# Attention and routed experts on one core: TensorE's program for 24 attention steps becomes a loop

## Chip, cores and metric

The kernel runs on one core of a Trainium2 chip. The metric is device time in microseconds, from one launch to its end. Each engine (TensorE for matmuls, VectorE, ScalarE, GpSimd, and SyncE, which issues DMAs) runs a program of its own; the programs meet at semaphores.

## What is computed

Attention inside chunks of 64 positions, then a two-level top-1 mixture of experts over the 4608 rows that attention gives.

```python
B, H, S, D = 8, 8, 576, 64; chunk = 64
scores = (1 / sqrt(D)) * matmul(q_c, k_c.T)          # per chunk of 64
attn = exp(scores - max); attn /= attn.sum(-1) + 1e-09
x = matmul(attn, v_c) -> (B * S, H * D) = (4608, 512)
g_idx = argmax(x @ w_group); g_w = softmax(...)[g_idx]           # 4 groups
e_idx = argmax(x[g] @ w_expert[g]); e_w = softmax(...)[e_idx]    # 4 experts in each
out[tok] = g_w * e_w * (relu(x[tok] @ w1[g, e]) @ w2[g, e])      # 512 -> 1024 -> 512
```

## The kernel before

The 4608 rows are 36 tiles of 128 rows, two chunks of 64 each. Four tiles make a group g, for which routing is done together. Attention runs as a software pipeline written out by hand: a recorder (R) takes every operation in one fixed order, puts it into the program of its engine, and works out from the memory that it reads and writes which semaphores it must wait for. Step t issues, in this order, work of several tiles:

- b(t+1), L578: scores of tile t+1 on TensorE, 16 matmuls of 64x64 (32 records, as f32 passes twice), into one of two score banks
- n(t-3), L622 to L633: VectorE divides the value product of tile t-3 by its sums and writes x
- s(t), L586 and L590: VectorE's maximum and subtraction for tile t
- c(t-1), L602: TensorE transposes the weights of tile t-1, ScalarE copies them (pT, L604)
- tile_e(t), L665 when t is odd, L672 when it is even: router matmuls, and ScalarE's copy of them
- p(t-2), L615: TensorE's product with v for tile t-2, into the one pair of output banks (ob)
- e(t): ScalarE's exponential (L596), and the exponential of routing (L691) when one is due
- x(t-3), L645: TensorE transposes x of tile t-3, ScalarE copies it (xT, L646)
- in one step of four the rank matmuls 3(g), L763 to L768, in one expert position for each row

Routing itself is a generator, route(g), then place(g), on VectorE; the calls more() slip one of its operations at a time between those of n and s, and four at a step's end. GpSimd scatters each finished tile to the memory of its experts (L801) and writes token numbers (L631). From step 24 on (EXTRA) the first expert's weights are loaded and split (F, P). Then come a written-out TAIL for the last tiles and a loop over expert tiles with branches by the tile's kind (L1144, L1128, L1090 and their second layers).

q and k come in pairs of tiles, 1 MB a load, into seven slots (NQ = 7); v comes three chunk columns a load into two buffers of nine (NV = 2). SyncE issues these loads in the recorder's order, each when its slot is free. The HEAD string is the order at the start, VS says at which step each v load stands.

TensorE's program for all of this is straight code, some 6,800 instructions. The class Pages plays it: it cuts the program into pages of 256 instructions, if it can in front of a b or p group with a wait, and jumps to the next page from there:

```python
if i > at and ops[i].stage and ops[i].waits:
    cut = i, n
...
if cut and cut[1] > room - SLACK and cut[1] < room:
    i, n = cut
...
self.pe.addr_align(PAGE, offset=0, max_nops=0)
```

## Time and profile before

| | us |
|---|---|
| median of three timed runs | 613.39 |
| lowest, highest | 613.26, 618.44 |
| profiled execution | 618.42 |
| its span, first to last instruction | 616.8 |
| TensorE busy (share of span) | 579.8 (94%) |
| VectorE busy | 360.8 (58%) |
| ScalarE busy | 263.3 (43%) |
| GpSimd busy | 158.2 (26%) |
| steps 9 to 32 of attention | 88.69 |

The profiled execution is one of its own, 5.0 us above the median. Its rows name the engine (PE is TensorE's matmuls, PEld its weight loads, DVE VectorE, ACT ScalarE, POOL GpSimd), the line of the kernel, what is written and read, and in brackets how long the engine stood idle before, with what released it as the view infers it. [...]

### The profile page before, as it was taken

The numbers are of one execution on the slowest core, as the hardware profiler recorded it, in microseconds if no ns is written. First come the engines' busy times: TensorE is split into PE (matmuls) and PEld (weight loads), VectorE is DVE, ScalarE is ACT, GpSimd is POOL, SyncE is SP. The second block draws the span as 40 slices with busy tenths as digits, with TensorE's granted clock in tenths as the row PEclk, the third lists the DMA queues.
The fourth block names the chain that finished last, engine by engine and source line by source line (L and its number), as shares of the span: only waits on it lengthen the run. The fifth ranks groups of instructions, "written<-read, shape, count | busy, mean of one in ns | idle before, by whom it ended". The sixth has DMA issues, their size and how long they took to land.

```text
span 616.8 us, 16000 instructions
## 1 busy us (share of the span) xinstructions
PE 579.8 (94%) x5711; PEld 498.9 (81%) x5712; DVE 360.8 (58%) x688; ACT 263.3 (43%) x367; POOL 158.2 (26%) x252
## 2 busy tenths in 40 slices
PE   7889979978998999999999999999999999999995
PEld 4666657756887989888889989889989988898984
DVE  4577869776767482136697474726326578763211
ACT  2455545756336241223685252626116355452111
POOL 0002314665403111212323312122111124321120
PEclk9899889997998999999999999999999999999999
DMA  7998997876549693118298763643613586921110
GB/s 280 422 312 277 352 366 240 243 228 207 163 146 395 240 330 109 39 30 296 103 348 311 261 245 121 221 153 113 236 51 123 208 323 223 331 105 64 34 44 24
DMA packets 43104, 128.27 MB, mean 208 GB/s; under 512 B 4590, under 2 KB 4974, under 8 KB 41136
## 3 DMA queue, kind: packets, MB, share of 16 engines
q1 hardware_dynamic: 32192, 93.93, 43.9%
q0 software_dynamic: 10864, 33.64, 15.5%
q8 instruction: 37, 0.61, 0.4%
q14 instruction: 11, 0.09, 0.1%
HBM read 106.40 MB, written 21.93 MB: 208 GB/s over the span
## 4 chain that ended last, share of the span: by engine, by line
PE 71%; DVE 11%; DMA 7%; issue 5%; POOL 2%; SPq 1%; ACT 1%; another core or an unknown queue 0%; DVEq 0%; POOLq 0%; ACTq 0%
PE banks L1159 28%; PE banks L1144 22%; PE banks L1128 4%; PE banks L615 2%; DVE x L633 2%; DVE pr L590 2%; DMA xgr<-xs 2%; DVE m L586 2%; DMA w1r<-in_moe_w_dram 2%; DMA qk<-in_qk_dram 2%; PE banks L471 2%; PE banks L602 2%; PE banks L1044 2%; PE banks L645 1%; PE banks L578 1%
## 5 line engine op out<-in xcount | busy, mean ns | idle before, releaser
L1144 PE MATMUL banks<-big,w1h 128*128 128x256 f32 x896 | 128.1, 283 | 1.4 <-issue 1.4
L1144 PEld LDWEIGHTS banks<-big,w1h 128*128 128x128 f32 x896 | 117.3, 192 | 2.9 <-issue 1.9
L1305 ACT ACTIVATE big<-banks 128x512 fp32r<-128x512 f32 x58 | 34.5, 596 | 158.9 <-PE banks L1144 126.0
L1159 PE MATMUL banks<-big,big 128*128 128x512 f32 x360 | 84.7, 393 | 0.0
L1635 POOL DMA_INDIRECT out_dram<-xl,io__154 x37 | 41.1, 1112 | 152.9 <-DVE xl L1371 144.4
L1159 PEld LDWEIGHTS banks<-big,big 128*128 128x128 f32 x360 | 66.5, 188 | 14.4 <-ACT big L1355 0.7
L1404 DVE SCALAR_TENSOR_TENSOR big<-banks,big 128x512 fp32r<-128x512 f32 x54 | 36.1, 687 | 64.3 <-ACT big L1305 62.0
L1159 PE MATMUL banks<-w2h,big 128*128 128x512 f32 x288 | 72.6, 399 | 0.2 <-ACT big L1305 0.2
L1144 PE MATMUL banks<-big,w1l 128*128 128x256 f32 x448 | 72.3, 283 | 0.6 <-DVE w1l L1381 0.6
L1381 DVE TENSOR_TENSOR w1l<-w1r,w1h 128x2048 fp32r<-128x2048 f32 x28 | 63.1, 2291 | 16.0 <-ACT w1h L1292 14.3
L1371 DVE TENSOR_SCALAR xl<-banks,io__154 128x512 f32<-128x512 f32 x33 | 24.7, 749 | 68.2 <-PE banks L1159 68.2
L1159 PEld LDWEIGHTS banks<-w2h,big 128*128 128x128 f32 x288 | 53.8, 190 | 12.2 <-ACT big L1305 0.9
L1144 PEld LDWEIGHTS banks<-big,w1l 128*128 128x128 f32 x448 | 61.9, 192 | 0.8 <-DVE w1l L1381 0.8
L1292 ACT CAST w1h<-w1r 128x2048 fp32r<-128x2048 f32 x28 | 52.2, 1903 | 7.8 <-DMA w1r<-in_moe_w_dram 6.0
L578 PE MATMUL banks<-qk 64*64 64x64 f32 x1152 | 27.8, 232 | 12.5 <-DMA qk<-in_qk_dram 3.5
L578 PEld LDWEIGHTS banks<-qk 64*64 64x64 f32 x1152 | 22.3, 141 | 20.8 <-DVE pr L590 4.5
L1385 DVE TENSOR_TENSOR w2l<-w2r,w2h 128x1024 fp32r<-128x1024 f32 x32 | 37.1, 1220 | 2.3 <-ACT w2h L1324 1.7
L1159 PE MATMUL banks<-w2l,big 128*128 128x512 f32 x144 | 35.6, 389 | 0.0
L604 ACT COPY pT<-banks 128x512 f32<-128x512 f32 x36 | 21.1, 586 | 33.6 <-PE banks L602 30.2
L615 PEld LDWEIGHTS banks<-va,pT 64*64 64x64 f32 x1152 | 21.4, 141 | 16.5 <-issue 4.8
L801 POOL DMA_INDIRECT xs<-x,pos x24 | 24.2, 1008 | 40.3 <-DVE pos L810 21.7
L1629 POOL COPY in__155<-xgr 128x2 int32<-128x2 int32 x22 | 10.7, 485 | 92.6 <-PE banks L1044 78.7
(223 smaller groups left out, 906.8 us busy)
## 6 DMA issues: line engine op xcount, KB each, us to landing
w1r<-in_moe_w_dram SPq DMA_DIRECT2D x30, 1024.0 KB
w2r<-in_moe_w_dram SPq DMA_DIRECT2D x30, 1024.0 KB
qk<-in_qk_dram SPq DMA_DIRECT2D x15, 1024.0 KB, 17.4
xgr<-xs POOLq DMA_DIRECT2D x38, 257.0 KB, 5.6
va<-in_v_dram SPq DMA_DIRECT2D x24, 390.0 KB
qk<-in_qk_dram SPq DMA_DIRECT2D x6, 512.0 KB, 8.7
w1r<-in_moe_w_dram POOLq DMA_DIRECT2D x2, 1024.0 KB, 9.4
w2r<-in_moe_w_dram POOLq DMA_DIRECT2D x2, 1024.0 KB, 8.2
```

What stands on the lines that cost most here:

```text
L578: R.tensor.matmul(sc[cols, x, hp * CH:hp * CH + CH], lhsT=T[rows, 0, hp, cols], rhs=T[rows, 1, hp, cols], start=True, stop=True)
L615: R.tensor.matmul(o[cols, x, hp * W:hp * W + W], lhsT=pT[rows, hp, cols], rhs=v_at(2 * t + c)[rows, hp], start=True, stop=True)
L1128: m = pe.matmul(ph[n], a_[:, c, 0:P], w_[:, c, n * 512:(n + 1) * 512], start=(i == 0), stop=(i == 11))
L1144: m = pe.matmul(ph[f // 2][:, f % 2 * 256:f % 2 * 256 + 256], w_[:, c, f * P:(f + 1) * P], a_[:, c, :], start=(i == 0), stop=(i == 11))
L1159: m = pe.matmul(py[j], a_[:, f, half[j]], w_(b, f), start=(i == 0), stop=(i == 23))
L1292: lambda b, s, j: ac.copy(wt[b][0][:, s], w1r[j]), K1)
L1305: ac.activation(hth()[:, 2 * b:2 * b + 2, :], ph[b].rearrange("p (f t) -> p f t", f=2), AF.Relu).then_inc(S["Ha"], 1)
L1371: return ve.tensor_scalar(out=yb[:, j, :], in0=py[j], scalar1=io_[:, j, 1:2], scalar2=None, op0=ALU.mult)
L1381: lambda b, s, j: ve.tensor_sub(wt[b][1][:, s], w1r[j], wt[b][0][:, s].bitcast(F32)), K1, js)
L1385: m = ve.tensor_sub(wt[b][4 + 2 * j + i], w2r[j][:, 2 * i:2 * i + 2], wt[b][2 + j][:, 2 * i:2 * i + 2].bitcast(F32))
L1404: ve.scalar_tensor_tensor(out=htl()[:, 2 * b:2 * b + 2, :], in0=ph[b].rearrange("p (f t) -> p f t", f=2), scalar=0.0, in1=hth()[:, 2 * b:2 ...
L1635: gp.indirect_dma_start(out, bass.IndirectOffsetOnAxis(ap=io[:, j, 0:1].bitcast(I32), axis=0), yb[:, j, :], None, bounds_check=N - 1, oob_ ...
```

## The change

TensorE's steps 9 to 32 are emitted once, as a loop of three turns of eight steps (play_turns). All operations must then be alike in each turn, or alike in turns of the same parity: stretches that differ stand in an if with two branches; these are the x transposes, since the x buffers of four groups fill two turns. Page cuts are gone; the loop starts on a page. Waits inside the loop can't count upward over turns, so they become tokens: take(name, o) makes the next TensorE operation wait until a semaphore of its own is 1 (16 for a DMA), and takes that much off it again; it stands in every turn, needed or not.

The tokens: BR, the score bank is free (VectorE's subtraction, passed on by ScalarE through a relay ahead of its exponential); XT, at c, ScalarE's copy of the x transposes of the step before; VX, at x, VectorE's x; PS and PT for the rank bank; the DMA of v at c of odd tiles, the DMA of the next q, k pair at p of even tiles.

So that turns are alike, the rings change: q and k in four slots (NQ = 4, 7 before), v in one ring of 16 chunk columns, four a load (NV = 16), its layout transposed on the host to match. HEAD and VS follow. In the step, p(t-2) is issued after x(t-3) instead of ahead of e(t).

In routing three operations of VectorE per group are folded. The comparison with the maximum (L707) goes into the next operation, which compares the difference with 0; the added 1e-9 (L743) becomes a fifth column of the exponentials; the running sum (L748) becomes a fifth row of the one-hot matrix (ohs), summed with it. The rank matmuls of odd groups have one small count matmul more.

```diff
-NV = 2
-NQ = 7
+NV = 16
+NQ = 4
+T0, T1, TURN = 9, 33, 8
 RE = RPE + 1
 XW = D + 2
 
...
-HEAD = "q0 I0 q1 V0 q2 q3 V1 q4 q5 V2 I1 G0 Q3 V3 Q4 V4 Q5 V5 Q6"
+HEAD = "q0 I0 q1 v0 q2 q3 v1 q4 q5 V1 I1 G0 Q3 V2 V3"
...
-VS = {}
-for _n in range(3 * NV, 3 * B):
-    VS.setdefault((3 * _n + 2 - 9 * NV) // 2 + 2, []).append(_n)
+VS = {2 * n - 5: (n,) for n in range(NV // 4, NT // 2)}
...
+    def take(self, name, o, via=None):
+
+        self.due.append((name, o, via))
+
+    def relay(self, eng, name, o):
+
+        op = Op(eng, None, None)
+        op.at, op.token, op.passes, op.line = len(self.ops[eng]), name, True, sys._getframe(1).f_lineno
+        self.want(op, [o])
         self.ops[eng].append(op)
...
-class Pages:
...
+    def play_turns(self, pe):
+        ops, turns = self.ops["tensor"], self.turns
+        first, n = ops.index(turns[0][0]), len(turns[0])
+        for op in ops[:first]:
+            self.emit("tensor", pe, op)
+        pe.addr_align(PAGE, offset=0, max_nops=0)
+        owed = []
+        with pe.Fori(0, len(turns)) as k:
+            odd = self.tc.nc.snap(k % 2, min_val=0, max_val=1)
+            at = 0
+            while at < n:
+                to, alike = at, turns[0][at].sig == turns[1][at].sig
+                while to < n and (turns[0][to].sig == turns[1][to].sig) == alike:
+                    to += 1
+                if alike:
+                    for op in turns[0][at:to]:
+                        self.emit("tensor", pe, op, owed)
                 else:
+                    with pe.If(odd == 0):
+                        for op in turns[0][at:to]:
+                            self.emit("tensor", pe, op, owed)
+                    with pe.Else():
+                        for op in turns[1][at:to]:
+                            self.emit("tensor", pe, op, owed)
+                at = to
+        for op in ops[first + n * len(turns):]:
+            self.emit("tensor", pe, op)
...
-                lane = "q%d" % (taken[0] % NQ)
-                st["T", n] = slot(qslots).rearrange("p (i z h t) -> p i z h t", i=2, z=2, h=4)
-                R.sync.dma_start(st["T", n], qk[n], lane=lane)
+                st["T", n] = qslots[n % NQ].rearrange("p (i z h t) -> p i z h t", i=2, z=2, h=4)
+                st["Q", n] = R.sync.dma_start(st["T", n], qk[n], lane="q%d" % (n % NQ))
...
-                return vbufs[b % NV][:, j]
-
-            def load_v(n):
-
-                b, i = divmod(n, 3)
-                R.sync.dma_start(vbufs[b % NV][:, 3 * i:3 * i + 3], v[b, :, 3 * i:3 * i + 3], lane="v%d" % (n % (3 * NV)))
+                return va[:, cc % NV]
+
+            def load_v(n, lo=0, hi=4, lane="v%d"):
+
+                i = 4 * n % NV
+                st["V", n] = R.sync.dma_start(va[:, i + lo:i + hi], v[:, 4 * n + lo:4 * n + hi], lane=lane % (n % (NV // 4)))
+
+            def load_v_half(i):
+
+                load_v(0, 2 * i, 2 * i + 2, "w%d%%d" % i)
 
...
                 T = st["T", t // 2][:, t % 2]
-                R.tensor.stage("b%d" % t)
                 sc = scb[t % 2]
+                if T0 < t <= T1:
+                    R.take("BR%d" % (t % 2), st[t - 2]["told"], st[t - 2]["sub"])
...
             def stage_exp(t):
                 pr = st[t]["pr"]
+                if T0 < t + 2 <= T1:
+                    st[t]["told"] = R.relay("scalar", "BR%d" % (t % 2), st[t]["sub"])
                 R.scalar.activation(pr, pr, AF.Exp, scale=0.125)
...
                 for hp in range(4):
+                    if T0 <= t + 1 < T1 and hp == 0:
+                        R.take("XT%d" % (t % 2), st[t - 3]["xt"])
+                    if T0 <= t + 1 < T1 and t % 2 and hp == 1:
+                        R.take("v%d" % (t // 2 % (NV // 4)), st["V", t // 2])
                     R.tensor.transpose(pt[:, hp, :], s["pr"][:, hp].rearrange("p x k -> p (x k)"), ident)
                 pT = apool.tile([P, 4, P], F32, name="pT")
-                R.scalar.copy(pT, pt)
+                s["pt"] = R.scalar.copy(pT, pt)
...
                 for hp in range(4):
                     for x, c, rows, cols in TILES:
+                        if T0 <= t + 3 <= T1 and t % 2 == 0 and (hp, x, c) == (1, 0, 0):
+                            R.take("q%d" % ((t // 2 + 2) % NQ), st["Q", t // 2 + 2])
                         R.tensor.matmul(o[cols, x, hp * W:hp * W + W], lhsT=pT[rows, hp, cols], rhs=v_at(2 * t + c)[rows, hp], start=True, stop=True)
...
                 for c in range(4):
+                    if T0 <= t + 3 < T1 and c == 0:
+                        R.take("VX%d" % (t % 2), st[t]["x_"])
                     R.tensor.transpose(pt[:, c, :], s["x"][:, c * P:(c + 1) * P], ident)
-                R.scalar.copy(st["xT", g][:, :, i * P:(i + 1) * P], pt)
+                s["xt"] = R.scalar.copy(st["xT", g][:, :, i * P:(i + 1) * P], pt)
 
...
+                        if T0 <= t + 4 < T1 and t % NG == 3 and c == 1:
+                            R.take("PS%d" % (t // NG % 2), st["ps", t // NG - 1])
                         R.tensor.matmul(e[32 * c:32 * c + 32, :], lhsT=wg[:, c, :], rhs=st["xT", g][:, c, i * P:i * P + 2 * P],
...
-                one = rpool.tile([P, R5, 4], F32, name="one")
-                V.tensor_tensor(out=by_t(one), in0=L, in1=by_t(mb), op=ALU.is_equal)
                 ls = rpool.tile([P, R5, 4], F32, name="ls")
                 V.tensor_tensor(out=by_t(ls), in0=L, in1=by_t(mb), op=ALU.subtract)
                 yield
 
-                io = cs[:, C_IOTA4:C_IOTA4 + 4].unsqueeze(1).broadcast_to([P, R5, 4])
-                V.scalar_tensor_tensor(out=one, in0=one, scalar=-64.0, in1=io, op0=ALU.mult, op1=ALU.add)
-                ex = rpool.tile([P, R5, 4], F32, name="ex")
-                st["ex"] = ex, ls
+                io = cs[:, C_I16:C_I16 + 4].unsqueeze(1).broadcast_to([P, R5, 4])
+                one = rpool.tile([P, R5, 4], F32, name="one")
+                V.scalar_tensor_tensor(out=one, in0=ls, scalar=0.0, in1=io, op0=ALU.is_equal, op1=ALU.mult)
+                ex = exs[g % 2]
+                st["ex"] = ex[:, :, 0:4], ls
...
-                        V.tensor_scalar(out=gt, in0=sv[:, :, 0:2], scalar1=1e-9, scalar2=None, op0=ALU.add)
+                        V.reciprocal(gt, sv[:, :, 0:2])
                     yield
-                with nc.allow_low_precision(reason="a sum of four ones and zeros"):
-                    V.tensor_reduce(out=cum[:, g + 1, :], in_=oh.rearrange("p t g e -> p (g e) t"), axis=AX.X, op=ALU.add)
-                V.reciprocal(gt, gt)
-                V.tensor_tensor(out=cum[:, g + 1, :], in0=cum[:, g + 1, :], in1=cum[:, g, :], op=ALU.add)
+                with nc.allow_low_precision(reason="a sum of ones and zeros, at most 36"):
+                    V.tensor_reduce(out=ohs[(g + 1) % 2][:, 0], in_=oh5.rearrange("p t e -> p e t"), axis=AX.X, op=ALU.add)
...
+                if T0 <= g * NG + 10 < T1:
+                    R.take("PT%d" % (g % 2), st[g * NG + 9]["pt"])
                 R.tensor.matmul(rk3, lhsT=one1, rhs=wide(cs[0:1, C_BASE:C_BASE + E], NG), start=True, stop=False)
-                R.tensor.matmul(rk3, lhsT=ones, rhs=wide(cum[:, g, :], NG), start=False, stop=False)
+                R.tensor.matmul(rk3, lhsT=ones, rhs=wide(ohs[g % 2][:, 0], NG), start=False, stop=False)
...
+                if g % 2 and g < GL - 1:
+                    n = rk[0:1, NG * E:NG * E + E]
+                    R.tensor.matmul(n, lhsT=ones[:, 0:1], rhs=ohs[(g + 1) % 2][:, 0], start=True, stop=True)
                 if g == GC:
...
                 for t in range(TL - 2):
+                    R.turn = (t - T0) // TURN if T0 <= t < T1 else None
                     run("b%d n%d s%d c%d" % (t + 1, t - 3, t, t - 1) if t > 2 else ("b1 s0", "c0 b2 s1", "p0 b3 s2 c1")[t])
                     if 4 <= t <= 4 + (GL - 1) * NG:
                         tile_e(t)
-                    run("p%d" % (t - 2) if t > 2 else "")
                     more(4)
                     run("e%d" % t)
                     stage_ex()
                     if t % 2 and t // 2 + NQ < NT // 2:
                         run("Q%d" % (t // 2 + NQ))
                     run("x%d" % (t - 3))
+                    run("p%d" % (t - 2) if t > 2 else "")
                     run(" ".join("V%d" % n for n in VS.get(t, ())))
                     if last(t - 7):
                         run("3%d" % ((t - 7) // NG))
                     run(EXTRA.get(t, ""))
+                R.turn = None
                 run(TAIL)
...
-                    Pages(pe, R).play(lambda op: R.emit("tensor", pe, op))
+                    R.play_turns(pe)
```

## Rows read from the trace of the kernel before

**Rows 1.** The 24 steps by windows: busy us (records), clock, DMA share, GB/s

```profile
45.73:48.72 2.99, 2.99 (x83) 2.11 (x81) 1.99 (x7) 1.58 (x4) 0.00 (x0) 1.00 0.96 295
48.72:51.50 2.78, 2.78 (x77) 2.45 (x76) 2.65 (x8) 1.94 (x5) 0.00 (x0) 1.00 0.65 253
51.50:54.50 3.00, 3.00 (x82) 2.12 (x81) 2.96 (x13) 1.91 (x5) 0.00 (x0) 1.00 0.62 140
54.50:57.98 3.48, 3.45 (x85) 2.94 (x84) 2.87 (x11) 2.04 (x5) 1.50 (x2) 1.00 0.94 278
57.98:64.84 6.86, 5.48 (x83) 3.47 (x81) 3.29 (x11) 2.18 (x5) 2.91 (x5) 0.77 1.00 401
...
84.90:89.38 4.48, 4.48 (x80) 2.98 (x80) 2.79 (x15) 1.49 (x3) 0.42 (x1) 0.62 0.98 398
...
sum 88.69, PE 78.34 PEld 60.26 DVE 67.22 ACT 48.76 POOL 32.07; mean PE 3.26 PEld 2.51 DVE 2.80 ACT 2.03 POOL 1.34
```

**Rows 2.** TensorE's timeline: start, length, engine, line, [idle before it <- releaser]

```profile
27.79 0.69 PE L578 MATMUL banks<-qk 64*64 64x64 f32 x32 [1.41 <-DVE m L586]
...
39.35 0.69 PE L578 MATMUL banks<-qk 64*64 64x64 f32 x32 [1.84 <-DVE x L633]
...
72.30 0.69 PE L578 MATMUL banks<-qk 64*64 64x64 f32 x32 [1.50 <-DVE pos L810]
...
79.15 0.70 PE L615 MATMUL banks<-va,pT 64*64 64x65 f32 x32 [1.62 <-issue]
...
84.90 0.69 PE L578 MATMUL banks<-qk 64*64 64x64 f32 x32 [1.68 <-DVE xl L633]
...
106.92 0.69 PE L578 MATMUL banks<-qk 64*64 64x64 f32 x32 [0.84 <-DVE ps L785]
...
112.50 0.70 PE L615 MATMUL banks<-va,pT 64*64 64x65 f32 x32 [0.95 <-DVE mx L702]
```

**Rows 3.** DMA queues in the 24 steps: packets, MB, share of 16 engines

```profile
q8 instruction: 16, 0.26, 1.3%
```

**Rows 4.** DMA queues from 69.80 to 70.90 us

```profile
q8 instruction: 1, 0.02, 5.7%
```

**Rows 5.** DMA packets from 16.5 to 39.35 us

```profile
DMA packets 1911, 9.39 MB, mean 411 GB/s; under 512 B 212, under 2 KB 274, under 8 KB 1058
```

**Rows 6.** VectorE's timeline near the end of the 24 steps

```profile
125.97 0.69 DVE L633 TENSOR_TENSOR x<-banks,rc 128x512 f32<-128x512 f32 x1 [2.42 <-POOL x L631]
```

**Rows 7.** All DMA queues that moved anything from 295 us to the end

```profile
q1 hardware_dynamic: 16000, 41.95, 36.9%
q0 software_dynamic: 4856, 13.82, 12.0%
```

**Rows 8.** The page's costliest groups: busy us, mean ns, idle before them

```profile
L1144 PE MATMUL banks<-big,w1h 128*128 128x256 f32 x896 | 128.1, 283 | 1.4 <-issue 1.4
```

**Rows 9.** Timeline of all engines around the step at 48.72

```profile
47.51 0.70 PE L615 MATMUL banks<-va,pT 64*64 64x65 f32 x32
...
50.10 0.69 DVE L590 TENSOR_TENSOR pr<-banks,m 128x512 f32<-128x512 f32 x1
...
50.83 0.63 ACT L596 ACTIVATE pr<-pr 128x512 f32<-128x512 f32 x1
...
51.45 0.27 ACT L691 ACTIVATE ex<-ls 128x80 f32<-128x80 f32 x1
...
51.62 0.57 ACT L646 COPY xT<-banks 128x512 f32<-128x512 f32 x1
...
52.13 0.66 PE L602 MATMUL banks<-cs,pr 128*128 128x128 f32 x4
```

**Rows 10.** The page's DMA issues: count, KB each, median us to landing

```profile
qk<-in_qk_dram SPq DMA_DIRECT2D x15, 1024.0 KB, 17.4
```

**Rows 11.** Groups by line in the 24 steps: busy us, mean ns, idle before

```profile
L707 DVE TENSOR_TENSOR one<-lg,mx 128x80 f32<-128x80 f32 x5 | 1.3, 264 | 0.2
...
L748 DVE TENSOR_TENSOR cum<-cum 128x16 bf16<-128x16 bf16 x6 | 1.0, 159 | 0.0
```

More of the change, by code (lines that the diff above doesn't have):

```diff
@@ L251, in number @@
         self.sem = dict(given)
+        self.turns = {}
+        for op in self.ops["tensor"]:
+            if op.turn is not None:
+                self.turns.setdefault(op.turn, []).append(op)
+        names = set(self.eaten)
+        for same in zip(*self.turns.values(), strict=True):
+            assert len({tuple(o.takes) for o in same}) == 1
+            for o in same:
+                o.inc = any(z.inc for z in same)
+                names.update(o.takes)
+        for e in self.ENGINES:
+            for op in self.ops[e]:
+                for i, (o, val) in enumerate(op.waits):
+                    if o.token and o.lane is None:
+                        o = next(z for z in self.ops[o.eng][o.at:] if z.token is None and z.lane is None and z.fn)
+                        assert o.eng != e or o.at < op.at, (op.line, o.line)
+                        op.waits[i] = o, val
+                        if o.turn is None:
+                            o.inc = True
+                        else:
+                            assert o.inc
         for e in self.ENGINES:
@@ L272, in emit @@
             z = op.fn(eng)
-        for w in last:
-            z._wait_ge(*self.wait(*w))
+        if owed and not op.inc and not last:
+            z.then_inc(*owed.pop(0))
+        for w, n in last:
+            z._wait_ge(*w)
+            if n:
+                owed.append((w[0], n))
         if op.lane is not None:
             z.then_inc(self.sem[op.lane], 16)
+        elif op.token:
+            z.then_inc(self.sem[op.token], 1)
         elif op.inc:
@@ L355, in f @@
             z.plain = True
-            if self.name == "tensor":
-                z.cost = 4 if op == "matmul" and named["lhsT"].dtype == F32 else 2
+            z.sig = (op,) + tuple((a.tensor.name, str(a.offset), str(list(a.ap)), str(a.dtype)) for a in writes + reads)
+            z.sig += tuple((k, v) for k, v in named.items() if isinstance(v, bool))
             return z
@@ L385, in moe_kernel @@
         pos8 = wpool.tile([P, NG], I32, name="pos8")
-        cum = wpool.tile([P, NG0 + 1, E], BF16, name="cum")
+        ohs = [wpool.tile([P, NG + 1, E], BF16, name="oh%d" % i) for i in range(2)]
         ones = wpool.tile([P, P], BF16, name="ones")
@@ L398, in moe_kernel @@
         slots, qslots = [], []
-        for i in range(NQ):
+        for i in range(7):
             at_ = wpool.at
```

129 lines of the change are left out of this document (69 added, 60 removed).

## The prediction

> **What bounds the kernel now.** I looked first at the clock and span of the core (618.4 us for the profiled execution, span 616.8, mean clock 0.982), then cut the 24 steps that the change turns into a loop at the start of each score group of TensorE (L578), read that table step by step, then TensorE's timeline for what stands before each group, then the DMA queues in narrow windows around the gaps, and last the timeline of all engines in steps where TensorE never waits.
>
> Four steps in a row run undisturbed [rows 1]: 2.99, 2.78, 3.00 and 3.48 us, 12.25 together, with TensorE busy for all but 0.03 of them and VectorE for 10.5 (1.99, 2.65, 2.96, 2.87). So TensorE sets the pace of these steps, and VectorE is the next limit, full only in the third. Six times 12.25 is 73.5 us; the 24 steps took 88.69. What has to be explained is the 15.2 us between.
>
> The idle time lies in front of some groups only [rows 2]: in the loop's steps five of them, at 72.30, 79.15, 84.90, 106.92 and 112.50, wait 1.50, 1.62, 1.68, 0.84 and 0.95 us, 6.6 together; ahead of them three, from 27.79 to 39.35 (those two stand in the rows), wait 1.41, 1.02 and 1.84, 4.3 together. The view names VectorE as the releaser of most, but VectorE's work had ended earlier or ended by chance; what these eight groups have in common is in the code. The class Pages cuts TensorE's program every 1.5 steps, in front of a score or a value group, and by its cuts all eight are the first of a page. The instruction queue agrees: 16 packets of 16 KB in the 24 steps, one for each 1.5 [rows 3]. One of them starts and ends between 69.80 and 70.90, and TensorE goes on at 72.30, 1.4 us after it [rows 4]; windows around the packets ahead of 79.15 and 84.90 give the same, three in all. So TensorE runs dry at a page's end whenever the packet is late. It is late where the DMA engines are full: from 16.5 to 39.35 they move 411 GB/s [rows 5], and there three of four page starts wait a microsecond or more. In the four undisturbed steps they move 140 to 295 [rows 1], and the page starts at 48.72 and 53.28 don't wait.
>
> Two more stretches belong to it. The step at 57.98 is a page's first too, and takes 6.86 us where 2.99 would do, 3.87 too much, partly at half clock (0.77 in the row). The step at 84.90 has no gap inside but a granted clock of 0.62 after the gaps ahead of it, and costs 4.48 for 2.99, 1.49 more [rows 1]. With the five gaps that is 12.0 of the 15.2. Of the rest 1.5 us is one wait at the end: VectorE stands 2.42 us until GpSimd, behind its weight work, writes a token number [rows 6].
>
> **The change part by part.** *The loop.* A turn holds eight steps. The four undisturbed steps hold 327 matmul and 322 weight-load records [rows 1], so a turn holds some 1,300 instructions, with the second branch's copies of the x transposes about 1,400, or 5.5 pages of 256. Three turns then need some six pages instead of 16, if the code stays. The row that bears on this is the experts' loop: from 295 us to the end the instruction queue moved nothing at all, only the two data queues stand in the list [rows 7], and by the program's instruction count that loop, all its branches taken again and again, is some 1,440 instructions, a little more than the new one. So the code of turns two and three should be there. Gain: the late pages of turns two and three all go. In the first turn, and in steps 3 to 8, pages still arrive one by one, but behind lighter traffic: the load order now starts with four q, k pairs and sixteen v columns instead of seven pairs and eighteen, then loads as it consumes. From the page starts that didn't wait under such traffic I keep only 0.9 of the 4.3 us ahead of the loop (gain 3.4; ends 0 and 4.3) and 1.5 us in the first turn (ends 0 and 3.9, which is what the step at 57.98 lost), and take the 12.0 as gone.
>
> [...]
>
> *Branches.* Eight if-branches a turn around the x transposes and one jump back. No row shows a branch in these steps. The nearest are the expert matmuls at L1144, in a loop with such branches: 1.4 us of idle with no releaser over 896 matmuls [rows 8]. Each branch here stands behind the c and e groups, already queued, which hide it; that cover is thin only where a turn ends behind a value group. Between 0 and 2.4 us (0.1 at each of 24); I take 0.5, near the row.
>
> *The new order and the new wait.* In the loop the x transposes go ahead of the value group, so a value group now ends its step. Everything that VectorE does for the next tile (n, then s) starts at that end. And the weight transposes (L602) of step t+1 now wait, in every step, for ScalarE's copy of the x transposes of step t (the XT token); before, they needed only the exponential. ScalarE's own order is weight copy, logit copy, exponential, then x copy, so that copy is its last work of a step. The undisturbed step at 48.72 gives the lengths [rows 9]: from the end of a value group (47.51 + 0.70 = 48.21) to the end of the subtract (50.10 + 0.69 = 50.79) 2.58 us; the exponential follows at 50.83 for 0.63; in one step of four the routing exponential follows (51.45, as soon as ScalarE is free); the x copy runs 51.62 to 52.19. Counted from the value group's end that is 3.98 us, 4.05 with the hand-over of 0.06. With the value group last, TensorE starts the next step right at that end and reaches the transposes after a step of 2.78 and a score group of 0.63 (51.50 to 52.13), at 3.41. It waits 0.64. Behind it in TensorE's queue are the transposes, e, x and the value group, and for that value group VectorE waits, so the delay is passed on. In the following step VectorE is full (2.96) and starts some 0.25 late, which makes another 0.2 to 0.3; in the step with the rank matmuls (3.48) and the one after it the slack covers it. I take 0.88 for four steps, 5.3 for 24. Ends: 0, if ScalarE is ahead of this timeline, and 1.75 for four, 10.5 in all, if the relay that ScalarE now carries for the score banks and the later start of VectorE add 0.1 in each step and both late steps double. This wait is next late when the pages are gone.
>
> *Rings.* q, k now run four pairs ahead, v eight tiles. A pair is issued some 6.5 steps, 21 us, before it is asked for, and lands in a median of 17.4 us when seven are in flight and the queue is full [rows 10]. Four steps need 2.1 MB of q and k, 1.06 of v and 1.05 of scattered tokens; over 13.1 us that is 320 GB/s, under the 411 of [rows 5]. I cost it at nothing; SP issues them in the order in which the slots come free, with one v load behind each q load.
>
> *Three routing operations folded* (the comparison, the added constant, the running sum): 0.26, 0.19 and 0.16 us, once in four steps (the first and the last of them in [rows 11]). VectorE has over 1.7 us free in four steps, and in the stretch where it is full the routing exponential starts when ScalarE is free, not when VectorE is. Nothing, at most 0.6 for four steps, 3.7 in all, should VectorE bind.
>
> **The sum.** Against the profiled execution: 618.4 - 3.4 - 12.0 + 1.5 + 0.5 + 5.3 = 610.3. That execution lies 5.0 us over the median of 613.4, and one of the three timed runs lies there too. If the 5.0 are gaps that the change takes away (the 3.87 at 57.98 looks like it), the changed kernel comes out at 610; if they lie elsewhere, at 605. I take 609.
>
> **The rivals.** (a) The x copy is not waited for: ScalarE's chain has more slack than the one step shows. Then 5.3 less: 604. For it, the copy was never in the way before; against it, the timeline leaves it 0.6 short. (b) The late pages are not what TensorE waits for, or the first turns and other waits fill the gaps: no gain, the new wait paid: 613.4 + 5.3 + 0.5 = 619. Against it stand the eight cuts and the packet times. (c) Slower: the loop's code is not kept. Every page is fetched as before, and at two jumps back the page is asked for only then. Two stalled page starts in a row are 5.75 us apart (79.15 and 84.90), so a page from asking to use costs up to that: 2 x 5.7 + 5.8 + 613.4 = 631. It decides from the point where a turn is longer than what stays; against it, the experts' loop. (d) The wait chain takes 1.75 for four steps: 5.2 more, 614.
>
> **How the numbers follow.** The forecast, 604 to 613 by its own ends, has 0.58; (a) 0.22, (d) 0.07, (b) 0.08, (c) 0.05. A measurement of this kernel can tell 1%, 6.1 us, from no change. Below 607.3 lie three tenths of the forecast and nearly all of (a): 0.37. Above 619.5 lie (c) and half of (b): 0.09. The rest, 0.54, is within 1%. For eight in ten the range goes from 600 to 618; it leaves out (c), half of (b) and the far end of (a).
>
> **What would show it.** Right: one instruction packet for each 1.5 steps in the first turn, none in the next two; no gap with a restart 1.4 us behind a packet; rank matmuls (L763) 13.1 us apart instead of 12.25 undisturbed or 14.8 (88.69 / 6) on average; the weight transposes released by ScalarE's x copy in the step after each routing exponential. Wrong: rank groups 12.3 apart (then a), instruction packets in the second turn (c), transposes waiting in every step (d), gaps as before with no packet near (b), or waits for q or v, which I cost at nothing.

## The result and the profile after

The changed kernel took 621.97 us (median of four, 619.87 to 623.55) where the kernel before took 613.33 beside it: a ratio of 1.014 [1.010, 1.018], slower by more than the 1% that can be told from no change. Run again later it took 626.03 beside 616.06, 1.013 [1.009, 1.017]. The forecast was 609, within 600 to 618. The kernel before is not always at 613: over five chips its median went from 610.9 to 616.9 and its runs on one chip spread over 6 to 11 us, so below each kernel is read against the kernel before that was timed beside it. A ratio and its interval leave out runs more than 1.5% above the fastest of the same kernel, which the median counts: a_no_jump's 620.9 and 626.9 (of twelve runs), a_all's 630.6 and 630.8 (of six; its median is 621.7 without them), and one run each of a_one_memset, a_ex_later and the kernel before in experiment 5.

The profiled execution of after took 621.43 us (span 619.8). Its attention looks much as forecast. In the timeline of TensorE (start, length, line, tile) the rank groups, one in four steps, answer to the steps of [rows 1]:

```profile
46.17 0.43 PE L848 MATMUL banks<-cs,one 1*128 1x64 f32 x2
62.34 0.43 PE L848 MATMUL banks<-cs,one 1*128 1x64 f32 x2
76.07 0.43 PE L848 MATMUL banks<-cs,one 1*128 1x64 f32 x2
89.01 0.43 PE L848 MATMUL banks<-cs,one 1*128 1x64 f32 x2
103.02 0.43 PE L848 MATMUL banks<-cs,one 1*128 1x64 f32 x2
120.29 0.43 PE L848 MATMUL banks<-cs,one 1*128 1x64 f32 x2
```

They lie 12.9 to 17.3 apart; before they lay 12.2 to 17.7 apart. The branch records of the loop put its three turns at 38.1, 69.6 and 95.8 us, its end at 127.2. The DMA queues in turns two and three, 69.85 to 127.24, carry one packet of code on q8, at 73.7, without a stop of TensorE there (packets, MB, share of the engines); before, [rows 3] had 16 for the 24 steps:

```profile
q1 hardware_dynamic: 1906, 10.10, 53.9%
q0 software_dynamic: 2216, 7.78, 39.5%
q8 instruction: 1, 0.02, 0.1%
q14 instruction: 2, 0.02, 0.1%
```

Two things went otherwise: a stop at the loop's entry and, long after attention, a chain from VectorE and GpSimd to TensorE in the experts' loop. They stand, with the new wait of the weight transposes, in the timeline of all engines (in brackets the idle time before and what ended it):

```profile
38.42 0.89 PE L647 MATMUL banks<-qk 64*64 64x64 f32 x21 [3.23 <-issue]
...
97.77 0.66 PE L677 MATMUL banks<-cs,pr 128*128 128x128 f32 x4 [0.64 <-ACT xT L724]
...
100.97 0.66 PE L677 MATMUL banks<-cs,pr 128*128 128x128 f32 x4 [0.30 <-ACT xT L724]
...
109.99 0.62 ACT L550 CAST w1h<-w1r 128x512 fp32r<-128x512 f32 x1 [3.02 <-DMA w1r<-in_moe_w_dram]
...
112.89 1.11 PE L677 MATMUL banks<-cs,pr 128*128 128x128 f32 x4 [2.13 <-ACT xT L724]
...
157.61 0.20 PE L1272 MATMUL banks<-cs,off 1*17 1x2 f32 x2
...
297.23 4.49 DVE L1469 TENSOR_TENSOR w1l<-w1r,w1h 128x2048 fp32r<-128x2048 f32 x2 [0.83 <-issue]
...
297.32 3.11 POOL L1723 DMA_INDIRECT out_dram<-xl,io__152  x1 [2.48 <-DVE xl L1465]
...
299.70 2.56 SPq L529 DMA_DIRECT2D w1r<-in_moe_w_dram  x2
...
300.43 0.55 POOL L1769 DMA_DIRECT2D word<-xs  x1
...
306.05 0.68 POOL L1717 COPY io__152<-in__153 128x2 int32<-128x2 int32 x1 [5.07 <-DMA word<-xs]
...
309.89 0.58 POOL L1712 DMA_DIRECT2D xgr<-xs  x1 [0.77 <-POOL in__153 L1718]
...
318.12 0.75 PE L1132 MATMUL banks<-identr,xgr 128*128 128x128 f32 x4 [5.36 <-DMA xgr<-xs]
```

The same places in the timeline of the kernel before (rows that the prediction didn't show):

```profile
162.65 0.20 PE L1184 MATMUL banks<-cs,off 1*17 1x2 f32 x2
...
302.30 2.33 DVE L1381 TENSOR_TENSOR w1l<-w1r,w1h 128x2048 fp32r<-128x2048 f32 x1 [0.91 <-issue]
...
302.30 1.03 POOL L1635 DMA_INDIRECT out_dram<-xl,io__154  x1 [2.21 <-DVE xl L1377]
303.34 0.55 POOL L1681 DMA_DIRECT2D word<-xs  x1
...
304.80 2.58 SPq L459 DMA_DIRECT2D w1r<-in_moe_w_dram  x2
...
308.35 0.58 POOL L1624 DMA_DIRECT2D xgr<-xs  x1 [0.77 <-POOL in__155 L1630]
...
315.44 2.32 POOL L1635 DMA_INDIRECT out_dram<-xl,io__154  x1 [5.77 <-DVE xl L1371]
...
317.43 0.89 PE L1044 MATMUL banks<-identr,xgr 128*128 128x128 f32 x8
...
507.40 3.09 POOL L1635 DMA_INDIRECT out_dram<-xl,io__154  x1 [2.80 <-DVE xl L1371]
```

L1272 (L1184 before) is the first matmul that builds the experts' tables, behind attention. I cut each profile there. In this pair after arrives 5.04 us earlier (157.61 for 162.65), and takes 462.2 us from there to the end where before took 454.1: 8.1 lost in code that the change doesn't touch, but for the buffer that one small matmul reads.

How: in a tile of few rows VectorE ends its output product, goes round its loop and subtracts w1l for the next tile; GpSimd scatters that product. Both set off from the same product. Before, both began at 302.30 and the scatter took 1.03. After, VectorE needed 0.83 instead of 0.91 and began at 297.23, the scatter came at 297.32 and took 3.11. The first of the two subtractions took 2.29 and ended at 299.52; the scatter ended 0.91 behind that, a little less than the 1.03 that it took before, as if it had been held until that end. (The scatter at 315.44 before began 0.89 into a subtraction, took 2.32 and ended 0.92 behind it.) Then the small transfer `word` goes out at 300.43, behind 1 MB of weights issued from 299.70 instead of ahead of them, GpSimd is held until 306.05 (5.07 us idle ahead of its copy, 1.42 before), the gather of the next rows is issued at 309.89, also behind weights (from issue to landing a median of 8.5 us, 5.0 before), and TensorE stands 5.36 us, where before it went on at 317.43 without a wait. A long scatter doesn't always cost that: the one at 507.40 before also took 3.09, and no wait of TensorE over 0.9 us follows it.

The lengths tell which of the two held the other. The scatter that began 0.09 us into the subtraction took 3.11 us for 1.03. In a_read_one (experiment 2) the subtraction began 0.34 us into a scatter and took its usual 2.29, and before, where the two began within 0.01 us, the scatter took 1.03 and the subtraction 2.33. So in these runs a subtraction under way held the scatter, and not the other way round.

### The profile page after: what moved, and what is told of

Read it like the earlier page. It is cut to its first block, busy times and chain, and to the rows that moved or that the text cites. A ratio compares the mean times of both kernels' runs of the same rounds, so it can differ in the third digit from the quotient of the medians.

```text
span 619.8 us, 16011 instructions
## 1 busy us (share of the span) xinstructions
PE 576.4 (93%) x5713; PEld 499.1 (81%) x5714; DVE 360.2 (58%) x663; ACT 262.0 (42%) x367; POOL 159.9 (26%) x252
## 3 DMA queue, kind: packets, MB, share of 16 engines
q0 software_dynamic: 10864, 33.64, 15.3%
## 4 chain that ended last, share of the span: by engine, by line
PE 72%; DMA 10%; issue 6%; DVE 5%; POOL 2%; ACT 1%; SPq 1%; POOLq 0%; DVEq 0%; ACTq 0%
PE banks L1247 29%; PE banks L1232 23%; DMA w1r<-in_moe_w_dram 4%; PE banks L1216 4%; DMA xgr<-xs 3%; PE banks L691 3%; PE banks L677 2%; PE banks L723 2%; PE banks L647 2%; PE banks L1132 2%; DMA out_dram<-xl,io__152 1%; PE banks L1178 1%; DMA xs<-xl,pos 1%; DMA word<-xs 1%; PE banks L745 1%
## 5 line engine op out<-in xcount | busy, mean ns | idle before, releaser
L1247 PEld LDWEIGHTS banks<-big,big 128*128 128x128 f32 x360 | 66.5, 188 | 14.3 <-ACT big L1443 0.7
L1473 DVE TENSOR_TENSOR big<-w2r,big 128x1024 fp32r<-128x1024 f32 x28 | 32.5, 1221 | 1.6 <-ACT big L1384 1.5
L887 POOL DMA_INDIRECT xs<-x,pos x24 | 24.7, 1030 | 33.2 <-DVE pos L896 17.3
```

The source lines that it names most:

```text
L887: R.gpsimd.do(lambda e: e.indirect_dma_start(xs, bass.IndirectOffsetOnAxis(ap=pos, axis=0), x, None), [pos, x, ("zeros", (0, 1, 0, 1)), (" ...
L1247: m = pe.matmul(py[j], a_[:, f, half[j]], w_(b, f), start=(i == 0), stop=(i == 23))
L1473: m = ve.tensor_sub(wt[b][4 + 2 * j + i], w2r[j][:, 2 * i:2 * i + 2], wt[b][2 + j][:, 2 * i:2 * i + 2].bitcast(F32))
```

## The experiments

Each kernel was timed 6 or 12 times beside the kernel before; a_short and b_short are read against each other. "Rest" is the time from the cut above to the end, in the profile. The expectations of the first runs call VectorE's time of 0.19 or 0.27 us between two branch records its jump back; it is the branch past the path that VectorE takes when the next tile has few rows (`If(k == 1)`, L1513 before), and the 0.08 us by which it differs is that of the 0.83 and 0.91 above.

**1. Is it VectorE's place in memory, or the race at all?** One memset fewer in after, one more in before; or the loop's register reads moved.

```diff
-for z in exs:                       # a_one_memset (after)
-    R.vector.memset(z[:, :, 4:5], 1e-9)
+R.vector.memset(exs[:, :, :, 4:5], 1e-9)
...
+R.vector.memset(one1, 1.0)          # b_one_more (before), twice
...
-read(cr, u + 1)                     # a_read_last, b_read_last: VectorE, ahead of YE
...
+read(cr, u + 1)                     # behind YE, at the turn's end
```

> The changed kernel with the two memsets of the ex tiles as one, so that VectorE's program has one instruction fewer ahead of the experts' loop and the loop lies where it lay in the kernel before (473 instructions of VectorE ahead of its common tail, 474 in the changed kernel). Nothing else differs. Theory 1, a lost race: in the changed kernel VectorE's jump back took 0.190 us instead of 0.271, its subtraction of w1 began 0.09 us ahead of GpSimd's scatter (at 297.23 and 297.32), the scatter then took 3.11 us instead of 1.03, the small transfer behind it landed behind the weights, and TensorE waited 7 us at 318; with the old place of the loop the race is won again: 622 - 7 = 615, between 613 and 617, and TensorE has no wait over 2 us for xgr near 318. Theory 2, the loss lies in TensorE's own placement or in the loads' earlier start, and the long scatter is an accident of one execution: 619 to 623.

> The kernel before with one memset of VectorE given twice, so that VectorE's experts' loop lies where it lies in the changed kernel (474 instructions ahead). Theory 1: the race is lost here too, up to 7 us: 617 to 621. Theory 2: no difference from before, 613 to 614.

> The changed kernel with VectorE's register loads for the next expert tile behind its output products instead of ahead of them, so that its next subtraction of w1 starts some 0.3 us later and GpSimd's scatter comes first whatever the place of the loop. Theory 1: 613 to 617, and no scatter over 1.2 us beside a subtraction of w1 that started in the same 0.2 us. Theory 2: 619 to 623, or up to 2 more, since VectorE starts 33 tiles later.

> The kernel before with VectorE's register loads for the next expert tile behind its output products. Theory 1: the scatter at 315 (2.32 us in the profile of before) wins too; 610 to 614, never above. Theory 2: 613 to 616.

Beside 616.89: a_one_memset 623.49 (1.010 [1.007, 1.013]), b_one_more 617.79 (1.001 [0.999, 1.003]), a_read_last 619.39 (1.003 [1.001, 1.006]), b_read_last 618.26 (1.003 [1.001, 1.005]). One instruction more or less moved nothing: the branch stayed short in the one and long in the other, and with it the scatter, 3.11 and 1.03. So the number of VectorE's instructions ahead isn't the cause; the race is not touched by that. Moving the reads won the race in after (rest 454.3, no wait for xgr), though the time stayed above theory 1's 617; in before it cost some 1.4 us, and against theory 1 the second scatter, at 314.28, still took 2.22.

**2. Attention alone, after once more, and a cheaper repair.** a_short and b_short set `nu = 6` in all engines, and SyncE waits for the weight loads at the end. a_read_one moves only the last of the three reads.

> The changed kernel with the experts' loop cut after five of its turns (six expert tiles in all; the rows of the other tiles are not computed or written), so that what is timed is attention, routing and the head of the experts. To be read against b_short, the same cut of the kernel before. Theory 1, attention gained and the experts' loop lost it: a_short is 2 to 5 us shorter than b_short. Theory 2, attention gained nothing in the typical run and the profile of after was a lucky one: within 1 us of b_short.

> The kernel before with the experts' loop cut after five of its turns (six expert tiles in all; the rows of the other tiles are not computed or written). Theory 1: 2 to 5 us longer than a_short. Theory 2: within 1 us of it. If the kernel before owes its spread of 7 us to attention, as gaps at late pages would, the spread shows here too; if to the experts' loop, its runs lie within 2 us.

> The changed kernel once more, beside the others on the same chip, for its spread and a second profile. Theory 1: 620 to 624, and in the profile the scatter of the fourth expert loop turn near 297 takes 3.1 us and TensorE waits 4 to 7 us for xgr behind it. Theory 2: 617 to 624, with or without that wait.

> The changed kernel with only the last of VectorE's three register loads for the next expert tile (0.43 us) behind its output products, so that the scatter near 297 comes ahead of the subtraction of w1 at a third of the cost of a_read_last. Theory 1: the wait of 4 to 7 us for xgr is gone as in a_read_last, and the time is 1 us or so below that kernel: 614 to 618 where the kernel before takes 617. Theory 2: as a_again.

a_short 297.80 (295.5 to 304.4), b_short 297.66 (295.8 to 302.1): no difference, theory 2. The 5 us of the first pair of profiles were luck, and attention brings its own spread. a_again 626.03, a_read_one 617.54 beside 616.06 (1.001 [0.998, 1.004]): one register read of VectorE gives 8.5 us back. Its timeline, VectorE's product and subtraction, GpSimd's scatter, TensorE without a wait:

```profile
300.88 0.74 DVE L1465 SCALAR_TENSOR_TENSOR xl<-banks,io__152,xl 64x512 f32<-64x512 f32 x1
302.88 2.29 DVE L1469 TENSOR_TENSOR w1l<-w1r,w1h 128x2048 fp32r<-128x2048 f32 x1 [1.26 <-issue]
...
302.54 1.04 POOL L1724 DMA_INDIRECT out_dram<-xl,io__152  x1 [2.09 <-DVE xl L1465]
...
318.04 0.89 PE L1132 MATMUL banks<-identr,xgr 128*128 128x128 f32 x8
```

**3. The counter-test, and the terms of attention.** b_late_scatter makes before lose; a_no_jump drops the page start ahead of the loop (on a_read_one); a_ex_later adds a later routing exponential; b_value_last is before with the new order alone.

```diff
 W("Y", u2 + (j + 1))                # b_late_scatter (before), GpSimd
+W("Y", u2 + (j + 1))
+W("Y", u2 + (j + 1))
...
-pe.addr_align(PAGE, offset=0, max_nops=0)   # a_no_jump, ahead of Fori
...
-stage_ex()                          # a_ex_later: ahead of run("x%d")
+stage_ex()                          # behind it
...
-run("p%d" % (t - 2) if t > 2 else "")       # b_value_last: ahead of more(4)
+run("p%d" % (t - 2) if t > 2 else "")       # behind run("x%d")
```

> The kernel before with GpSimd asking two more times for the semaphore that it has just waited for, ahead of each scatter of the experts' loop: some 0.15 us later, nothing else. Theory 1, the race between that scatter and VectorE's subtraction costs the changed kernel its 4 to 8 us: the kernel before now loses it too, the scatter near 303 takes 3.1 us, TensorE waits 3 us or more for xgr behind it, and the time goes from 616.5 to between 620 and 625. Theory 2, the long scatter only goes along with something else: 616 to 618.

> a_read_one without the jump to a page's start ahead of the attention loop. Theory 1: the stop of 3.2 to 5.1 us in front of the loop's first score group (38 to 40 us in five profiles of the changed kernel, 1.6 to 1.8 at that step before) is the page that the jump asks for only when it gets there; it falls to under 1.8, the half clock behind it goes too, and the time is 2 to 4 us below a_read_one: 613 to 615.5 where the kernel before takes 616.5. Theory 2: the page is late with or without the jump, or the loop's own set-up takes the time: 617 to 618. Theory 3: the loop, which now begins inside a page, no longer stays in place, and pages come in turns two and three: 620 or more.

> a_no_jump with ScalarE's routing exponential behind the copy of the x transposes instead of ahead of it, one step in four. Theory 1: the weight transposes wait 0.3 us less for that copy after each routing exponential, rank groups of turns two and three go from 14.0 to 13.7 apart, 1 to 2 us less than a_no_jump. Theory 2: the wait moves to the step behind, since the exponential then delays that step's copies: the same as a_no_jump within 1.

> The kernel before with only the new order: the value group behind the x transposes in every step, as the loop has it, in straight code with its pages and rings. Theory 1, as the forecast had it: TensorE's step then ends with the group that VectorE waits for, the transposes wait for ScalarE, and four undisturbed steps take 0.9 more, 14.1 where rank groups lay 13.2 apart; the time goes from 616.5 to between 619 and 622. Theory 2: that wait belongs to the loop's own semaphore for the x copy, and straight code has it only where the bank asks for it: rank groups 13.2 to 13.5 apart, 615 to 618.

Beside 614.92: b_late_scatter 623.46, 1.012 [1.008, 1.017]. Theory 1: with VectorE as before (0.91) and only GpSimd later, 0.09 us by the distance from the product's end (0.92 before, 1.01 here), the old kernel shows the whole loss:

```profile
300.29 4.49 DVE L1381 TENSOR_TENSOR w1l<-w1r,w1h 128x2048 fp32r<-128x2048 f32 x2 [0.91 <-issue]
...
300.39 3.10 POOL L1637 DMA_INDIRECT out_dram<-xl,io__154  x1 [2.39 <-DVE xl L1377]
...
320.55 0.75 PE L1044 MATMUL banks<-identr,xgr 128*128 128x128 f32 x4 [4.90 <-DMA xgr<-xs]
```

a_no_jump 614.05, 0.997 [0.994, 1.000], where a_read_one had 1.001. The stop at the loop's entry is gone, and so is the half clock behind it. Windows of 5.08 us from the loop's first score group, in after and in a_no_jump (busy of each engine, then clock, DMA share, GB/s), and that group in a_no_jump's timeline, without idle time ahead:

```profile
38.42:43.50 5.08, 5.08 (x80) 3.49 (x84) 0.20 (x2) 2.07 (x4) 0.00 (x0) 0.50 0.61 239
```

```profile
35.81:40.89 5.08, 4.16 (x118) 3.14 (x118) 4.91 (x21) 3.32 (x7) 0.00 (x0) 1.00 0.98 289
```

```profile
35.81 0.69 PE L646 MATMUL banks<-qk 64*64 64x64 f32 x32
```

Its turns two and three, from 65.1 on, had one packet of code too, at 65.8, and no more; so theory 3 falls. a_ex_later 613.35, 0.997 [0.994, 1.001]: theory 2, no gain; rank groups stay 14.0 apart in its undisturbed block, as in a_no_jump.

b_value_last 620.12, 1.007 [1.004, 1.010]: the time that theory 1 named, but not by its mechanism. The four steps without a late page took 13.4 between rank groups, the block behind it 15.3, and among TensorE's waits from 60 to 125 us none is for ScalarE's copy ahead of the weight transposes (L602); the score groups (L578) wait, as at page starts before (engine, line, releaser; us, times, longest):

```profile
PE banks L578 <- DVE x L633: 2.5, 1, 2.5
PE banks L578 <- DVE ps L785: 2.1, 2, 1.0
PE banks L578 <- DVE pr L590: 1.2, 3, 0.9
```

One profile doesn't settle why the order costs 5 us in straight code.

**4. Which part tips the race?** b_fold is before with the three folded operations alone, b_rings before with the rings, HEAD and VS alone; a_word_first and a_all try to repair after at GpSimd.

```diff
-gp scatter(2 * u + 2, 0)            # a_word_first: ahead of If(k > 1)
 with gp.If(k > 1):
+    scatter(2 * u + 2, 0)
     scatter(2 * u + 2, 1)
 with gp.Else():
     gp.dma_start(word, ...)
+    scatter(2 * u + 2, 0)
```

> The kernel before with only the three routing operations folded. In all profiles so far VectorE's branch by the tile's kind took 0.13 us between two branch records in kernels with the changed attention and 0.21 in kernels with the old one, and by that 0.08 us the race with GpSimd's scatter is lost or won. Theory 1, the folded operations, the only part of the change in VectorE's own program, move that branch: 0.13, a scatter of 3.1 us near 300, 620 to 625. Theory 2, another part moves it: 0.21, no such scatter, 614 to 617, as the forecast had it for this part (nothing).

> The kernel before with only the new rings: four slots for q and k, sixteen columns of v, the new order of the first loads, v laid out by column. Theory 1 of the forecast: nothing, 614 to 617 (and 3.4 us gained ahead of step 9 at best, 612 to 613, if lighter traffic makes pages there arrive in time). Theory 2: the rings are what the changed kernel is late by at its first rank group (1.5 us): 616 to 619, the first rank group at 46 instead of 44.7, and waits for q, k or v in the steps behind. If VectorE's branch takes 0.13 us here, the rings move it: 620 or more.

> The changed kernel with GpSimd issuing the small transfer of a tile of few rows ahead of that tile's scatter instead of behind it, which also takes the branch between the two out of the scatter's way. Theory 1: the scatter comes some 0.1 to 0.2 us earlier and wins the race: 1.0 us near 297, no wait for xgr, 615 to 618. Theory 2: it still loses (3.1 us); then the time tells which landing held GpSimd up: 616 to 619 if it was the small transfer's, which now goes out before the weights, 621 to 624 if it is the scatter's own.

> The changed kernel with the small transfer ahead of the scatter, without the jump ahead of the loop, and with the routing exponential behind the copy of the x transposes. Where the kernel before takes 615 to 617: 611 to 613 if the race is won and VectorE's register reads need no delay; 614 as a_no_jump if the win only moves elsewhere in the experts' loop; 618 or more if the race is still lost.

Beside 615.89: b_fold 625.74, 1.015 [1.010, 1.019]. Theory 1: three small operations a group fewer, with two memsets more and other buffers for them, and the kernel before loses all of it and more. Its timeline is that of after:

```profile
301.84 4.49 DVE L1383 TENSOR_TENSOR w1l<-w1r,w1h 128x2048 fp32r<-128x2048 f32 x2 [0.83 <-issue]
301.93 3.11 POOL L1637 DMA_INDIRECT out_dram<-xl,io__153  x1 [2.06 <-DVE xl L1379]
...
323.08 0.75 PE L1046 MATMUL banks<-identr,xgr 128*128 128x128 f32 x4 [5.70 <-DMA xgr<-xs]
```

b_rings 618.48, 1.005 [1.001, 1.008]: its scatter won (rest 451.6), yet it is some 2.6 us slower; its first rank group came at 45.2, inside the range of before, so where the rings cost that is open. a_word_first 622.59 (1.012 [1.007, 1.017]): theory 2, and in its second half: the scatter still came 0.09 behind the subtraction (3.13 us) although `word` had left at 301.50, so GpSimd is held by the scatter's own landing:

```profile
311.06 1.25 POOL L1717 COPY io__152<-in__153 128x2 int32<-128x2 int32 x1 [5.08 <-DMA out_dram<-xl,io__152]
```

a_all 624.94 (1.011 [1.005, 1.018]): still lost.

**5. Give b_fold 0.1 us back.** `W("TB", 1)` twice ahead of `prep1(code, [0])` on VectorE; a_two_waits has the same in after without the jump and with the later exponential.

> b_fold (the kernel before with the folded operations alone) with VectorE asking twice for a semaphore that it has long had, in the path of a tile of few rows, ahead of the subtraction of w1: 0.1 us or so later, no other change. Theory 1, those 0.1 us against GpSimd's scatter are all that the folded operations cost: the scatter near 302 takes 1.0 us again and the time falls from 625.7 to between 614 and 618. Theory 2, the folded operations cost something else as well: 619 or more, with a short scatter.

> The changed kernel without the jump ahead of the loop, with the routing exponential behind the copy of the x transposes, and with VectorE's two waits as in b_fold_waits in the place of the register read of a_ex_later: 612 to 614 where the kernel before takes 615 to 616, or 622 and more if the race is still lost.

Beside 610.93: 619.61 (1.013 [1.008, 1.018]) and 617.09 (1.012 [1.006, 1.018]). The edit missed the place: the waits stand in the path for a next tile of few rows, `If(k == 1)`, while the subtraction that meets the scatter here runs in the Else behind it. VectorE still began 0.83 behind its product, and both scatters lasted 3.1. Later in the loop, where the waits did run, they did what was meant. There the kernel b_fold has a scatter 0.10 behind the subtraction:

```profile
514.78 2.29 DVE L1383 TENSOR_TENSOR w1l<-w1r,w1h 128x2048 fp32r<-128x2048 f32 x1 [0.80 <-issue]
...
514.88 3.09 POOL L1637 DMA_INDIRECT out_dram<-xl,io__153  x1 [2.79 <-DVE xl L1373]
```

In b_fold_waits the subtraction begins 0.10 later behind its product, and the scatter is short:

```profile
511.60 2.33 DVE L1383 TENSOR_TENSOR w1l<-w1r,w1h 128x2048 fp32r<-128x2048 f32 x1 [0.90 <-issue]
...
511.60 1.02 POOL L1639 DMA_INDIRECT out_dram<-xl,io__153  x1 [2.80 <-DVE xl L1373]
```

At that place TensorE has no wait over 0.9 us either way. So whether the folded operations cost anything besides the race stays untested.

## Why the prediction was wrong

The profiles of all these kernels, with a scatter of 1.0 or of 3.1 us at that one place, fall into two sets by their rest. Won (before, b_one_more, b_read_last, b_rings, b_value_last, a_read_last, a_read_one, a_no_jump, a_ex_later): 451.6 to 455.8, mean 453.6. Lost (after, a_again, a_one_memset, a_word_first, a_all, a_two_waits, b_late_scatter, b_fold, b_fold_waits): 458.1 to 464.7, mean 460.9. No overlap, 7.3 us apart, and kernels with the old and the new attention are in both sets. In all nine of the lost TensorE waits 2.9 to 5.7 us for xgr at that place; in the won no such wait reaches 0.9.

Attention in the same profiles (without a_two_waits and b_fold_waits, timed on a chip where attention is shorter in both: 153 and 156 us):

| us | before's, 6 profiles | after's, 7 | without the jump, 3 | forecast, to before |
|---|---|---|---|---|
| to the first rank group | 44.9 | 46.2 | 42.6 | -3.4 |
| its five blocks of four steps | 75.8 | 72.2 | 71.1 | -4.7 for six |
| from there to the experts | 42.6 | 43.0 | 43.8 | 0 |
| sum | 163.3 | 161.4 | 157.5 | -8.1 |

Before's are before, b_one_more, b_read_last, b_short, b_late_scatter, b_fold; after's are after, a_one_memset, a_read_last, a_again, a_read_one, a_short, a_word_first; then a_no_jump, a_ex_later, a_all.

- **The step that failed: "Three routing operations folded ... Nothing, at most 0.6 for four steps, 3.7 in all, should VectorE bind."** Alone it cost 9.85 us (b_fold), of which 7.3 are the lost race by the two sets. I priced the instructions where they stand, and took the 454 us behind attention to follow one to one; they hold a choice that 0.1 us decides. No rival had it either.
- **Ahead of the loop, a gain of 3.4:** a loss of 1.3. The jump to a page for the loop, which I cost at nothing, stopped TensorE for 3.1 to 5.1 us in seven profiles (3.23 in after, 3.28 in a_read_one, 3.62 in a_again, 5.07 in a_short), where before the gap at that step was 1.84 [rows 2]; over the 5.1 us behind it the granted clock was 0.50 to 0.69 in the seven (0.50 in after), and 1.00 in the four kernels without the jump. Without it the gain is 2.3. Within the stop one packet of code came (35.5 in after), though no row says that it held the jump's target. At the two jumps back of the loop in after TensorE didn't stop: one packet came 4.1 us behind the first and none behind the second.
- **Late pages, 12.0 gained; first turn 1.5 and branches 0.5 lost:** right in kind. Blocks two and three fell from 17.8 and 16.9 to 15.1 and 13.4 (means of the six and seven profiles), the first rose from 13.1 to 14.6. The first turn cost more than the 1.5: in after its eight steps took 31.5 us by the branch records, with packets still coming and the half clock behind the entry in it, where the second turn took 26.2. The 0.5 for branches was an estimate; from 69.9 to 98 us in after, the second turn and 2 us of the third, TensorE waits 2.0 us for the x copy and 0.2 for ScalarE's relay, and no wait is put down to a branch. Rival (c) is refuted by the queue in after.
- **The new wait, 5.3 (0.88 for four steps):** right in size. In after TensorE waits 2.0 us for the x copy from 69 to 98 us, two blocks of 14, and rank groups of the fourth block lie 14.1 apart, 13.4 before. The forecast of 13.1 apart was met in the second turn (26.2 for its eight steps) and missed in the third (31.4). There ScalarE stands 3.02 us at its cast of the first expert's weights (109.99) until they land, its copies for attention queue behind it, and TensorE waits 2.13 for the x copy at 112.89, a wait that the code now hangs on that engine in every step. That is one execution: the block took 17.3 in it and 14.3 to 15.7 in the other six profiles. Five blocks together gained 3.6, 4.7 without the jump, and the forecast had 4.7 for its six.
- **Rings at nothing:** 2.6 us [0.7, 4.8 by the interval's ends] in straight code.
- **The 5.0 us between the profiled run and the median** was no sign of anything: 29 runs of the kernel before on one chip fill 613.9 to 621.5.

Together: 8.1 expected of attention; 1.9 got by the profiles, which isn't told from nothing (the six spread over 5.6 us, the seven over 7.5, and the timed short kernels differ by 0.1); and 7.3 lost to the race. That makes after 5.4 slower, where the medians say 8.6 and 10.0: the other 3 to 5 us have no cause here. The median came 13.0 above the forecast, which lay only 4.3 below the kernel before, since the 8.1 were taken for the most part off the profiled execution. With the race won after is level with before (a_read_one, 1.001). Without the jump as well, it is the only version here that may be ahead: 0.997 [0.994, 1.000] for a_no_jump, [0.994, 1.001] with the later exponential, at the edge of what can be told.

Left open: why the branch past that path took 0.08 us less in every kernel with the folded operations (by VectorE's count of instructions it is not); where the rings and the new order lose time in straight code; and a scatter clear of the subtractions by a wait on it was not tried.

## What to carry to other kernels

A loop downstream can hold a race between engines whose loser pays in microseconds: here a scatter 0.09 us late took 3.11 us for 1.03, and the two sets lie 7.3 us apart. Look for two instructions that start within 0.1 us of each other off one releaser, and order them on purpose, before reading a gain upstream. A change in time of a part that the diff doesn't touch is found by cutting both traces at the same instruction and aligning what follows. An edit that is to delay one instruction has to be found in the trace ahead of that instruction: the waits of experiment 5 ran on another path. And one pair of profiles isn't a measurement of a stage: here it showed attention 5 us faster where seven against six showed 1.9, and the timed short kernels no difference.

## What the runs showed of the hardware

- A scatter of GpSimd took 1.02 to 1.04 us when it began 0.34 us ahead of VectorE's subtraction w1l<-w1r,w1h (a_read_one), level with it (b_fold_waits, 511.60) or 0.005 us behind its start (before, 302.30). It took 3.09 to 3.13 us when it began 0.09 to 0.10 behind (after, a_word_first, b_late_scatter, b_fold and b_fold_waits at the place of the race; before at 507.40, after at 510.26, b_fold at 514.88), and 2.32 when 0.89 behind (before, 315.44). Begun 0.09 to 0.89 us behind, it ended 0.90 to 0.93 us behind the subtraction, which itself took 2.28 to 2.33 in either order.
- One branch of VectorE, over the same instructions, took 0.13 us to its next record in after and 0.21 in before, each of the six times that it was taken (0.03 the other three). The subtraction behind it began 0.83 us behind its product in after, a_word_first, b_fold and b_fold_waits, and 0.91 in before and b_late_scatter.
- The jump to a page ahead of the loop stopped TensorE for 3.23 us in after, 3.28 in a_read_one, 3.62 in a_again and 5.07 in a_short. Over the 5.08 us behind it in after the granted clock was 0.50; in a_no_jump, without the jump, TensorE had no idle time there and the clock was 1.00. In after the loop of some 1,400 instructions (an estimate from its records) ran two more turns, 69.85 to 127.24 us, on a single packet of code.
- Two waits that were already satisfied moved what stood behind them by 0.09 to 0.10 us: GpSimd's scatter from 0.92 to 1.01 behind the product (before, b_late_scatter), VectorE's subtraction from 0.80 to 0.90 behind it (b_fold at 514.78, b_fold_waits at 511.60).
